# Spectral sums by accumulating transfers from GpSimd instead of load, add and store

## The chip, the core and the metric

The kernel runs on one core of one Trainium2 chip. The metric is the device time of one execution in microseconds (us). Of the kernel before, three runs took 2753.51 to 2755.38 us, the median is 2754.12 us. Engines are named as in the profile: PE (TensorE), DVE (VectorE), ACT (ScalarE), POOL (GpSimd) and SP (SyncE, which here issues transfers).

## The reference

Two independent results stand side by side in the output of 2048 x 2048 fp32. Columns 0 to 1023 are an attention with 32 heads that share one key and one value head:

```python
q = (x @ wq).reshape(B, S, H, Dh).transpose(0, 2, 1, 3)      # S 2048, H 32, Dh 32
k, v = x @ wk, x @ wv
p = softmax(einsum("bhqd,bkd->bhqk", q, k) * Dh ** -0.5)
a = einsum("bhqk,bkd->bhqd", p, v).transpose(0, 2, 1, 3).reshape(B, S, H * Dh) @ wo
```

Columns 1024 to 2047 are a Fourier mixing, the part that the change touches:

```python
a = einsum("bsd,ed->bse", x, dft_hid_re)
b = einsum("bsd,ed->bse", x, dft_hid_im)
y = einsum("ts,bse->bte", dft_seq_re, a) - einsum("ts,bse->bte", dft_seq_im, b)
```

## The kernel before

The large matrix products (both stages of the Fourier mixing, and the last product with `wo`) are done in Strassen's way: `PRODUCTS` (line 30) lists seven products of blocks in place of eight. Each takes a signed sum of left blocks and of right blocks, and its result goes with a sign into one or two of four result blocks. So most results are sums of several products, and each of the 12 entries (product, result block) past the first of its block is an addition to what stands there already.

Stage 1 (`stage_1`, line 381) makes the hidden transform in the order `ORDER_1` = 4, 1, 2, 3, 0, 6, 5; each product has 8 row blocks of 128 rows and 2 column halves, so 16 groups. Its sums are kept in DRAM tiles of 128 x 512 fp32 called `a` (256 KB each). Stage 2 (`stage_2`, line 405) multiplies by the sequence matrices in the order `ORDER_2` with 8 groups a product; its partial sums stand in DRAM tiles `y`, and the last addition goes into the output. Stage 3 is the product with `wo`.

A group accumulates in one of two PSUM banks (`psb`). Every operand is split into a high part (DVE: `mh`, `rh`) and a low part (POOL or DVE: `ml`, `rl`), and three matmuls make one exact product. When a group is done, `gather` (line 351) copies the bank to an SBUF tile `h` on DVE. `h` comes from a ring of three buffers (`hr`, `NHR` = 3). A first entry is stored from `h` by SP. A first entry with a minus sign is copied a second time, times -1 (line 368). For any other entry SP loads the old sum to a tile `y` (ring of four), POOL adds or subtracts `h` (line 377), and SP stores `y` (line 379). There are 128 such additions in stage 1 and 64 in stage 2.

The attention runs between these groups. PE computes rows of scores into `pss` (two buffers of 128 x 1024), DVE takes their maximum (`nm`, line 727), ACT takes the exponent with its sum, which frees the buffer (line 729); PE computes the scores again transposed (`pst`), ACT takes their exponent to `p`, and PE multiplies `p` by `v` in bursts. A row's PE pair waits for the exponent of the row but one before (`row_deps`, line 899).

The order of all instructions is set while the program is built. `Plan` (line 67) keeps for every engine but PE the tasks whose inputs it expects to be there, with guessed durations, and picks by priority; the main loop (line 1040) picks PE's next work against the same clock. Each engine then executes its list strictly in order, and waits on semaphores where an input or a buffer is late. A ring slot may be taken in the plan once the users of the slot three before are finished in the plan; which of the three buffers a new tile gets is settled when it is made (`Ring.make`, line 161). Line numbers in the trace are nearly all L58, the helper that records every instruction, so the trace is read by tile names.

Of the kernel before, what the change touches and what calls it, by code (L numbers as in the profile page):

```python
# [12 lines left out]
ALU = mybir.AluOpType  # L13
# [4 lines left out]
P = 128  # L18
S = 2048
D = 1024  # L20
H = 32
DH = 32
W = 512
# [20 lines left out]
EXTRA = 2  # L44
OVER = {"act": 0.1, "dve": 0.08, "pool": 0.06, "sp": 0.0}
LAG = {"act": 0.1, "dve": 0.1, "pool": 0.15, "sp": 0.3, "pe": 0.1}
ISSUE, RATE, FLIGHT = 0.42, 300.0, 3.0


class Ordered:  # L50
# [16 lines left out]
class Plan:  # L67
# [6 lines left out]
        self.port = {"dve": 0.0, "pool": 0.0}  # L74
        self.seq, self.dma = 0, 0.0

    def task(self, engines, us, emit, deps=(), prio=0.0, kb=0, order=(), into=None, port=False):
        if isinstance(engines, str):
            engines = ((engines, 0.0),)
        t = into or Task()  # L80
        t.engines, t.us, t.emit, t.prio, t.kb, t.port = engines, us, emit, prio, kb, port
        self.seq += 1
        t.seq = self.seq
        for kind, ds in ((0, deps), (1, order)):
            for d in ds:
                if d is None:
                    continue
                if d.end is None:
                    t.n += 1
                    d.outs.append((t, kind))  # L90
                else:
                    t.ready = max(t.ready, d.start if kind else d.end)
        if t.n == 0:
            self.learn(t)
        return t
# [23 lines left out]
    def run(self, until):  # L119
        while True:  # L120
            best = self.next()
            if best is None or best[0] > until:
                return
            at, e = best
            r, t = min((x for x in self.known[e] if x[0] <= at), key=lambda x: (x[1].prio, x[1].seq))
            for f, _ in t.engines:
                self.known[f] = [x for x in self.known[f] if x[1] is not t]
            t.on = e
            t.emit(e) if len(t.engines) > 1 else t.emit()
            us = t.us[e] if isinstance(t.us, dict) else t.us  # L130
            if e == "pool" or (e == "dve" and t.port):
                at = max(at, self.port["dve" if e == "pool" else "pool"])
                self.port[e] = at + us - OVER[e]
            end = at + us
            self.free[e] = max(end - OVER[e], at + us / 2)
            if e == "sp":
                self.dma = max(self.dma, end) + t.kb / RATE
                end = self.dma + FLIGHT
            self.finish(t, at, end)


class Slot:
# [45 lines left out]
def tile_kernel(ctx: ExitStack, tc, xT, wq, wkv, wo, xbT, wT, cT, out):  # L188
# [3 lines left out]
    dve = Ordered(tc, nc.vector)  # L192
    gp = Ordered(tc, nc.gpsimd)
    sp = Ordered(tc, nc.sync)
    eng = {"act": act, "dve": dve, "pool": gp}
    scale = float(DH) ** -0.5
    plan = Plan()
# [7 lines left out]
    def scratch(name, shape=(P, W)):  # L205
        return dram.tile(list(shape), F32, name=name)
# [8 lines left out]
    y_d = [[[scratch(f"y_{t}_{e}_{k}") for k in range(8)] for e in range(2)] for t in range(2)]  # L215
# [27 lines left out]
    yr = Ring(misc, "y", NY, [P, W], F32)  # L243
    hr = Ring(misc, "h", NHR, [P, W], F32)
# [15 lines left out]
    def maker(ring, *a, **k):  # L260
        t = plan.task(*a, order=ring.maker, **k)
        ring.maker = [t]
        return t


    landed = defaultdict(Task)

    def store(to, of, deps, prio, kb=256, key=None, bits=False):
        return plan.task("sp", ISSUE, lambda: (move if bits else sp.dma_start)(to(), of()), deps=deps, prio=prio, kb=kb,
                         into=landed[key] if key else None)  # L270
# [71 lines left out]
    def totals():  # L342
        total = {}
        for _, _, outs in PRODUCTS:
            for i, j, _ in outs:
                total[i, j] = total.get((i, j), 0) + 1
        return total

    TOTAL = totals()

    def gather(g, at, outs, neg=False):

        s = hr.take()

        def evict():
            h = hr.make(s)
            if neg:
                dve.tensor_scalar_mul(h, g.ps, -1.0)
            else:
                dve.tensor_copy(h, g.ps)  # L360
        e = g.freed = maker(hr, "dve", 0.69, evict, deps=[g.done, *s.deps], prio=-0.5)
        for sg, key, n, to, of in outs:
            if of is None and sg > 0:
                s.users.append(store(to, lambda: s.tile, [e], at, key=(*key, n)))
                continue
            if of is None:
                s2 = hr.take()
                g.freed = maker(hr, "dve", 0.69, lambda s2=s2: dve.tensor_scalar_mul(hr.make(s2), g.ps, -1.0),
                                deps=[g.done, *s2.deps], prio=-0.5)
                s2.users.append(store(to, lambda s2=s2: s2.tile, [g.freed], at, key=(*key, n)))  # L370
                continue
            ys = yr.take()
            ld = plan.task("sp", ISSUE, lambda ys=ys, of=of: sp.dma_start(yr.make(ys), of()),
                           deps=[landed[*key, n - 1], *ys.deps], prio=at - 30, kb=256, order=yr.maker)
            yr.maker = [ld]
            f = gp.tensor_add if sg > 0 else gp.tensor_sub
            ad = plan.task("pool", 1.33, lambda ys=ys, f=f: f(ys.tile, ys.tile, s.tile), deps=[e, ld], prio=at - 20)
            s.users.append(ad)
            ys.users.append(store(to, lambda ys=ys: ys.tile, [ad], at, key=(*key, n)))

    def stage_1():
        seen = {}
# [22 lines left out]
    def stage_2():  # L405
        seen = {}
        for p in ORDER_2:
            at, bt, outs = PRODUCTS[p]
            R = [Item([(lambda r=r, e=e, c=c: a_d[r][e][c], sg) for r, e, sg in bt],
                      after=[("a", c // 8, r, c % 8, e, TOTAL[c // 8, r]) for r, e, sg in bt],  # L410
                      sums=scratch(f"as_{p}_{c}") if len(bt) > 1 else None) for c in range(NC)]
            for m in range(8):
                L = [Item([(lambda r=r, i=i, c=c, m=m: cT[r, i * 8 + m, :, c * 4:c * 4 + 4], sg) for r, i, sg in at])
                     for c in range(4)]
                got = []
                for i, j, sg in outs:
                    n = seen[i, j, m] = seen.get((i, j, m), 0) + 1
                    r0 = (i * 8 + m) * P
                    to = out[r0:r0 + P, D + j * W:D + (j + 1) * W] if n == TOTAL[i, j] else y_d[i][j][m]
                    got.append((sg, ("y", i, j, m), n, lambda to=to: to,  # L420
                                (lambda i=i, j=j, m=m: y_d[i][j][m]) if n > 1 else None))
                yield Group(L, R, lambda g, at, got=got: gather(g, at, got))

    def wo_set(e):
# [91 lines left out]
    rest = x_groups(1, False, True) + x_groups(2, False, True) + x_groups(3, False, True)  # L516
    rest += list(stage_1())
    rest += list(stage_2())
    WO = sum(g.n for g in start + rest)
    rest += list(stage_3())  # L520
# [321 lines left out]
    def at_of(deps):  # L842

        t = 0.0
        for d in deps:
            if d is None:
                continue
            if d.end is None:
                return None
            t = max(t, d.end + LAG["pe"])  # L850
        return t
# [17 lines left out]
    def product_deps(g, j):  # L869
        c, w = divmod(j, 3)  # L870
        l, r = g.left[c // 4], g.right[c]
        deps = [l.ready[0], r.ready[0]] if w == 0 else [r.ready[1]] if w == 1 else [l.ready[1]]
        if j == 0:
            deps.append(bank_task[other_bank()])
            deps += [o.done for o in odds if o.must <= fill]
        return deps
# [22 lines left out]
    def row_deps(s):  # L899
        u = s // SU  # L900
        return [*unit[u].open, *(kvs[:6] if s < EARLY else kvs), *([rexp[s - 2]] if s > 1 else [])]
# [14 lines left out]
    def col_deps(n):  # L916
        return [*unit[n // SU].rows, *([cexp[n - 1]] if n else [])]
# [11 lines left out]
    def pv_deps(k):  # L929
        u, q = flat[k]  # L930
        return [cexp[u * SU + 2 * bursts[u][q][1] - 1], bank_task[other_bank()]]
# [49 lines left out]
    def place():  # L981
        g = at_group[fill]
        return g, fill - g.at
# [40 lines left out]
    s = k = 0  # L1024
# [14 lines left out]
    n, after_burst, spare_0 = 0, False, None  # L1039
    while n < total:  # L1040
# [11 lines left out]
        elif k < len(flat) and n >= scored(k):  # L1052
            t = at_of(pv_deps(k))
# [13 lines left out]
        if after_burst:  # L1067
            after_burst = False
            t = at_of(row_deps(s)) if SU + LEAD <= s < min(n + SU + LEAD + RUN, total) else None
# [4 lines left out]
        if n and fill < BODY:  # L1074
            if spare_0 is None:
                spare_0 = spare()
            if spare() > spare_0 * (total - n) / total + SPARE_END:
                t = at_of(product_deps(*place()))
# [3 lines left out]
        if s >= min(n + SU + LEAD, total) and n < scored(k) + (held[0] is not None):  # L1082
            t = at_of(col_deps(n))
# [5 lines left out]
        if s < min(n + SU + LEAD + RUN, total) and (s >= SU + LEAD or fill >= min(s_at(s), BODY)):  # L1089
            t = at_of(row_deps(s))  # L1090
# [6 lines left out]
        if fill < BODY:  # L1097
            t = at_of(product_deps(*place()))
# [96 lines left out]
```

## Time and profile before

| | us |
|---|---|
| median of three runs | 2754.12 |
| the profiled execution, its own time | 2754.33 |
| its span from first to last instruction | 2752.5 |
| PE busy in the span | 2736.0 |
| ACT, DVE, POOL busy | 2199.5, 1944.1, 1579.5 |
| POOL's additions of spectral sums (192) | 249.3 |

The profiled execution lies within the three runs. PE is busy nearly all the time at a granted clock of 0.999, so an engine's busy time tells little: what counts is whether PE ever waits. Stage 1 of the Fourier part lies between about 350 and 1027 us, stage 2 between 1027 and 2480 us, and stage 3 and the end follow. Within stage 1, the third product (2) has its 16 groups between about 545 and 640 us.

### The profile page before, as it was taken

To read this page: it belongs to the slowest core of one execution; us is meant where nothing else is said; L and a number is where in the kernel's file an instruction comes from. 1 tells how busy PE (TensorE), PEld (TensorE's weight loads), DVE (VectorE), ACT (ScalarE), POOL (GpSimd) and SP (SyncE) were. 2 spreads that over 40 slices of the span, in tenths; PEclk is the share of its full clock that TensorE was granted. 3 is DMA by queue.
4 is the path that set the end of the run, shared out by engine and by line. 5 is a ranking of instruction groups with operands and counts; after the bars stand their busy time and mean duration, and the time that the engine had idled before them with its cause. 6 is when DMAs were issued, how large, how long until landed. Compare 5 with 4: busy or idle time off the path is not lost.

```text
span 2752.5 us, 40883 instructions
## 1 busy us (share of the span) xinstructions
PE 2736.0 (99%) x13832; PEld 1930.3 (70%) x13832; DVE 1944.1 (71%) x2277; ACT 2199.5 (80%) x3197; POOL 1579.5 (57%) x1307
## 2 busy tenths in 40 slices
PE   9999999999999999999999999999999999999999
PEld 6777676767676767677677676676676776766766
DVE  8977676768777776676677677677677676678752
ACT  6688887878787878888888888888888888887631
POOL 2644245557776557556346356557768767555562
PEclk9999999999999999999999999999999999999999
DMA  9645366567786548547437445547858857444585
GB/s 279 210 135 159 104 202 207 191 231 256 249 257 222 169 149 281 171 133 250 141 106 249 143 136 174 154 153 254 272 182 279 278 161 238 127 127 153 160 277 176
DMA packets 337043, 536.48 MB, mean 195 GB/s; under 512 B 36800, under 2 KB 89536, under 8 KB 336832
## 3 DMA queue, kind: packets, MB, share of 16 engines
q1 hardware_dynamic: 336832, 533.87, 61.3%
q8 instruction: 108, 1.77, 0.3%
q14 instruction: 103, 0.84, 0.1%
HBM read 390.86 MB, written 141.82 MB: 194 GB/s over the span
## 4 chain that ended last, share of the span: by engine, by line
PE 97%; ACT 1%; DVE 1%; DMA 1%; issue 0%; POOL 0%; SPq 0%; ACTq 0%; DVEq 0%
PE psb L58 62%; PE pss L58 18%; PE pst L58 17%; ACT pss L58 0%; ACT p L58 0%; DMA qst<-in_xT_dram 0%; DVE h L58 0%; DMA ql<-y 0%; DVE nm L58 0%; DVE rl L58 0%; DMA m<-in_wkv_dram 0%; DVE y L58 0%; ACT h L58 0%; POOL rl L58 0%; DVE p L58 0%
## 5 line engine op out<-in xcount | busy, mean ns | idle before, releaser
L58 DVE TENSOR_REDUCE nm<-pss 128x1 f32<-128x1024 f32 x1024 | 1241.6, 1221 | 325.0 <-PE pss L58 321.2
L58 ACT ACTIVATE p<-pst 128x1024 f32<-128x1024 f32 x1024 | 1052.5, 1028 | 448.6 <-PE pst L58 397.7
L58 ACT ACTIVATE pss<-pss,nm 128x1024 f32<-128x1024 f32 x1024 | 1110.7, 1085 | 35.0 <-DVE nm L58 33.6
L58 POOL TENSOR_TENSOR ml<-m,mh 128x512 fp32r<-128x512 f32 x371 | 482.6, 1301 | 508.2 <-DVE mh L58 290.9
L58 PE MATMUL psb<-rl,mh 128*128 128x512 f32 x1732 | 683.3, 395 | 0.6 <-POOL rl L58 0.6
L58 PE MATMUL psb<-rh,mh 128*128 128x512 f32 x1732 | 683.7, 395 | 0.2 <-DVE y L58 0.2
L58 PE MATMUL psb<-rh,ml 128*128 128x512 f32 x1732 | 683.3, 394 | 0.0
L58 PE MATMUL pss<-kst,qst 128*128 128x512 f32 x2048 | 650.4, 398 | 0.9 <-ACT pss L58 0.9
L58 PE MATMUL pst<-qst,kst 128*128 128x512 f32 x2048 | 642.8, 395 | 2.4 <-ACT p L58 2.2
L58 PEld LDWEIGHTS pss<-kst,qst 128*128 128x128 f32 x2048 | 375.6, 188 | 163.6 <-issue 72.9
L58 PE MATMUL psb<-p,v 128*32 128x512 f32 x4096 | 461.8, 596 | 2.7 <-DVE h L58 2.7
L58 PEld LDWEIGHTS pst<-qst,kst 128*128 128x128 f32 x2048 | 382.5, 188 | 103.1 <-ACT p L58 8.6
L58 POOL TENSOR_TENSOR m<-m,m 128x512 f32<-128x512 f32 x230 | 301.0, 1309 | 152.4 <-DMA m<-in_cT_dram 93.8
L58 PEld LDWEIGHTS psb<-rh,mh 128*128 128x128 f32 x1732 | 324.9, 188 | 77.7 <-DVE y L58 0.6
L58 PEld LDWEIGHTS psb<-rl,mh 128*128 128x128 f32 x1732 | 324.9, 188 | 76.6 <-POOL rl L58 1.0
L58 PEld LDWEIGHTS psb<-rh,ml 128*128 128x128 f32 x1732 | 324.9, 188 | 75.7
L58 POOL TENSOR_TENSOR y<-y,h 128x512 f32<-128x512 f32 x192 | 249.3, 1306 | 176.8 <-DVE h L58 165.1
L58 PEld LDWEIGHTS psb<-p,v 128*32 128x32 f32 x4096 | 122.7, 110 | 286.5 <-issue 273.7
L58 POOL TENSOR_TENSOR rl<-r,rh 128x512 fp32r<-128x512 f32 x198 | 255.7, 1299 | 117.6 <-DVE rh L58 108.5
L58 DVE TENSOR_REDUCE mh<-m 128x512 fp32r<-128x512 f32 x371 | 250.7, 676 | 20.5 <-PE psb L58 13.8
L58 ACT ACTIVATION_READ_ACCUMULATOR pss<-pss,nm 128x1 f32 x1024 | 208.2, 203 | 0.0
L58 POOL TENSOR_TENSOR r<-r,r 128x512 f32<-128x512 f32 x140 | 180.5, 1293 | 47.8 <-DMA r<-a 31.1
(78 smaller groups left out, 977.0 us busy)
## 6 DMA issues: line engine op xcount, KB each, us to landing
m<-in_cT_dram SPq DMA_DIRECT2D x384, 256.0 KB, 3.8
r<-a SPq DMA_DIRECT2D x192, 256.0 KB, 4.2
y<-a SPq DMA_DIRECT2D x128, 256.0 KB, 3.7
a<-y SPq DMA_DIRECT2D x128, 256.0 KB, 3.2
r<-in_wT_dram SPq DMA_DIRECT2D x96, 256.0 KB, 3.9
m<-in_xbT_dram SPq DMA_DIRECT2D x96, 256.0 KB, 3.3
y<-y SPq DMA_DIRECT2D x96, 256.0 KB, 4.1
as<-r SPq DMA_DIRECT2D x80, 256.0 KB, 4.4
```

Of the source, the lines that this page charges most:

```text
L58: return lambda *a, **k: self.tc.keep_in_program_order(f(*a, **k))
```

## The change

Additions to a sum that stands in DRAM are no longer made by load, add and store. GpSimd issues one transfer per addition, which reads the SBUF tile `h` and adds it to the DRAM tile (`accum_op=ALU.add`). Where the entry has a minus sign, DVE makes a second copy of the bank, times -1, in another slot of the `h` ring, and that tile is added. In stage 2 all entries go straight into the output; the DRAM tiles `y` are not used. The plan takes 1.0 us on POOL for such a task (`ACC`) and regards its result as landed, and the `h` slot as free, `FLIGHT + 1.0` = 4 us later. The rest is as it was.

```diff
-ISSUE, RATE, FLIGHT = 0.42, 300.0, 3.0
+ISSUE, RATE, FLIGHT, ACC = 0.42, 300.0, 3.0, 1.0
...
-            self.finish(t, at, end)
+            self.finish(t, at, end + t.after)
...
-            ys = yr.take()
-            ld = plan.task("sp", ISSUE, lambda ys=ys, of=of: sp.dma_start(yr.make(ys), of()),
-                           deps=[landed[*key, n - 1], *ys.deps], prio=at - 30, kb=256, order=yr.maker)
-            yr.maker = [ld]
-            f = gp.tensor_add if sg > 0 else gp.tensor_sub
-            ad = plan.task("pool", 1.33, lambda ys=ys, f=f: f(ys.tile, ys.tile, s.tile), deps=[e, ld], prio=at - 20)
-            s.users.append(ad)
-            ys.users.append(store(to, lambda ys=ys: ys.tile, [ad], at, key=(*key, n)))
+            if sg < 0:
+                s2 = hr.take()
+                e2 = g.freed = maker(hr, "dve", 0.69, lambda s2=s2: dve.tensor_scalar_mul(hr.make(s2), g.ps, -1.0),
+                                     deps=[g.done, *s2.deps], prio=-0.5)
+            else:
+                s2, e2 = s, e
+            s2.users.append(plan.task("pool", ACC, lambda s2=s2, to=to: gp.dma_start(to(), s2.tile, accum_op=ALU.add),
+                                      deps=[e2, landed[*key, n - 1]], prio=at - 20, into=landed[*key, n], after=FLIGHT + 1.0))
...
-                    to = out[r0:r0 + P, D + j * W:D + (j + 1) * W] if n == TOTAL[i, j] else y_d[i][j][m]
+                    to = out[r0:r0 + P, D + j * W:D + (j + 1) * W]
```

With other durations the plan comes out in another order. Two places in product 2 of stage 1 show it, where every group is stored once with plus (tile `a_0`) and added once with minus (tile `a_1`). In these rows the numbers tell tiles apart; DMAHW0 to 7 are semaphores of SP's transfers, DMASW0 to 7 those of POOL's.

The first place is DVE about the groups of row blocks 13 and 14. Before, each group has one copy `h`:

```order
L58 TENSOR_REDUCE nm_6067<-pss_6111 128x1 [waits PE_49]
L58 TENSOR_REDUCE nm_6067<-pss_6133 128x1 [waits PE_49]
L58 COPY h_6151<-psb_6103 128x512 [waits DMAHW3_49,PE_49]
L58 COPY mt_6160<-psb_6149 48x128 [waits PE_49]
L58 TENSOR_REDUCE nm_6067<-pss_6153 128x1 [waits PE_49]
L58 TENSOR_REDUCE mh_6189<-m0_5876 128x4x128
L58 TENSOR_TENSOR ov_5960<-ov_5960,psb_6165 128x512 [waits PE_49]
L58 TENSOR_REDUCE nm_6067<-pss_6202 128x1 [waits PE_49]
L58 TENSOR_REDUCE nm_6067<-pss_6210 128x1 [waits PE_49]
L58 TENSOR_REDUCE nm_6067<-pss_6233 128x1 [waits PE_49]
L58 COPY h_6249<-psb_6215 128x512 [waits DMAHW5_49,PE_49]
L58 TENSOR_REDUCE nm_6067<-pss_6252 128x1 [waits PE_49]
```

Now each has two, the second one times -1 (TENSOR_SCALAR):

```order
L58 TENSOR_SCALAR h_6113<-psb_6042 128x512 [waits DMAHW2_49,DVE_49]
L58 TENSOR_REDUCE mh_6119<-m0_5836 128x4x128
L58 TENSOR_REDUCE nm_5997<-pss_6116 128x1 [waits PE_49]
L58 COPY h_6154<-psb_6099 128x512 [waits DMASW2_49,DVE_49,PE_49]
L58 TENSOR_SCALAR h_6161<-psb_6099 128x512 [waits DMASW3_49,DVE_49]
L58 TENSOR_TENSOR ov_5907<-ov_5907,psb_6133 128x512 [waits PE_49]
L58 TENSOR_REDUCE nm_5997<-pss_6164 128x1 [waits PE_49]
L58 TENSOR_REDUCE nm_5997<-pss_6191 128x1 [waits PE_49]
L58 COPY h_6206<-psb_6172 128x512 [waits DMASW4_49,DVE_49,PE_49]
L58 TENSOR_SCALAR h_6212<-psb_6172 128x512 [waits DMAHW7_49]
```

A group's copies have come to two, and the second copies `h_6161` and the next first copy `h_6206` wait for semaphores of POOL's transfers. The second place is POOL beside it. Before, POOL adds `h` to a loaded `y`:

```order
L58 TENSOR_TENSOR m0_6091<-m0_6091,m1_6096 128x512 [waits DMAHW1_49,DMAHW0_49,Pool_49]
L58 TENSOR_TENSOR y_5974<-y_5974,h_6151 128x512 [waits DMAHW6_49,DMAHW2_49,DVE_49]
L58 TENSOR_TENSOR ml_6190<-m0_5876,mh_6189 128x512 [waits DVE_49,PE_49]
L58 TENSOR_TENSOR m0_6198<-m0_6198,m1_6200 128x512 [waits DMAHW4_49,DMAHW3_49,Pool_49]
L58 TENSOR_TENSOR y_6070<-y_6070,h_6249 128x512 [waits DMAHW6_49,DVE_49]
L58 TENSOR_TENSOR y_6130<-y_6130,h_6287 128x512 [waits DMAHW7_49,DVE_49]
L58 TENSOR_TENSOR ml_6306<-m0_5951,mh_6305 128x512 [waits DVE_49,PE_49]
```

Now it issues a transfer of the negated tile, each on the next of eight semaphores (it waits there for the transfer eight before):

```order
L58 TENSOR_TENSOR m0_6048<-m0_6048,m1_6056 128x512 [waits DMAHW3_49,DMAHW1_49,Pool_49]
L58 DMA a_1_1_13_243<-h_6113 128x512 [waits DMASW3_49,DVE_49]
L58 TENSOR_TENSOR ml_6120<-m0_5836,mh_6119 128x512 [waits DVE_49,PE_49]
L58 DMA a_1_0_14_228<-h_6161 128x512 [waits DMASW4_49,DVE_49]
L58 TENSOR_TENSOR m0_6156<-m0_6156,m1_6159 128x512 [waits DMAHW2_49,DMAHW0_49,Pool_49]
L58 DMA a_1_1_14_244<-h_6212 128x512 [waits DMASW5_49,DVE_49]
L58 TENSOR_TENSOR ml_6228<-m0_5899,mh_6227 128x512 [waits DVE_49,PE_49]
```

The addition's place in POOL's list is taken by the transfer; the one of `h_6113` uses DMASW3, that of `h_6161` DMASW4, so those are what the two DVE copies above wait for.

## Rows read from the trace of the kernel before

**Rows 1.** The page's first lines: the span, and engines' busy time and instructions.

```profile
span 2752.5 us, 40883 instructions
...
PE 2736.0 (99%) x13832; PEld 1930.3 (70%) x13832; DVE 1944.1 (71%) x2277; ACT 2199.5 (80%) x3197; POOL 1579.5 (57%) x1307
```

**Rows 2.** The page's chain that ended last, shares by engine.

```profile
PE 97%; ACT 1%; DVE 1%; DMA 1%; issue 0%; POOL 0%; SPq 0%; ACTq 0%; DVEq 0%
```

**Rows 3.** Stretches: length, busy PE, PEld, DVE, ACT, POOL, clock, DMA share, GB/s.

```profile
545.00:640.00 95.00, 95.00 (x496) 65.69 (x495) 67.54 (x80) 76.55 (x111) 57.60 (x47) 1.00 0.70 230
640.00:1027.00 387.00, 385.47 (x1951) 273.02 (x1953) 286.06 (x331) 315.29 (x457) 263.32 (x217) 1.00 0.68 218
```

**Rows 4.** Costliest groups, whole run: busy us, mean ns, idle before, releaser.

```profile
L58 DVE TENSOR_REDUCE nm<-pss 128x1 f32<-128x1024 f32 x1024 | 1241.6, 1221 | 325.0 <-PE pss L58 321.2
...
L58 POOL TENSOR_TENSOR y<-y,h 128x512 f32<-128x512 f32 x192 | 249.3, 1306 | 176.8 <-DVE h L58 165.1
```

**Rows 5.** Groups of DVE between 545 and 640 us.

```profile
L58 DVE TENSOR_REDUCE nm<-pss 128x1 f32<-128x1024 f32 x37 | 44.8, 1219 | 12.5 <-PE pss L58 12.5
...
L58 DVE COPY h<-psb 128x512 f32<-128x512 f32 x16 | 11.0, 690 | 4.3 <-issue 1.9 <-PE psb L58 1.4 <-DMA qst<-ql 0.5
L58 DVE TENSOR_REDUCE mh<-m 128x512 fp32r<-128x512 f32 x8 | 5.4, 674 | 0.0
...
L58 DVE TENSOR_TENSOR rl<-r,rh 128x512 fp32r<-128x512 f32 x4 | 3.3, 834 | 0.1
L58 DVE TENSOR_TENSOR ov<-ov,psb 128x512 f32<-128x512 f32 x3 | 2.1, 686 | 6.6 <-PE psb L58 6.6
```

**Rows 6.** DMA, 545 to 640 us: busy tenths in 40 slices; issues, median landing.

```profile
DMA  6999999988996469748303236884492032659999
...
y<-a SPq DMA_DIRECT2D x16, 256.0 KB, 3.9
a<-h SPq DMA_DIRECT2D x16, 256.0 KB, 3.3
a<-y SPq DMA_DIRECT2D x16, 256.0 KB, 3.3
```

**Rows 7.** The page's DMA queues: packets, MB, share of 16 engines.

```profile
q1 hardware_dynamic: 336832, 533.87, 61.3%
```

**Rows 8.** Tile y: its stores' issue on SP, who waited for it, its landings.

```profile
L58 SPq DMA_DIRECT2D a<-y x128: 319/326/1330, 449.4 to 1028.1; - x128
...
  PEld psb L58: 0.6, 1
  PE psb L58: 0.2, 1
...
DMA to landing us min/median/max: 2.0/3.5/8.4
```

**Rows 9.** Waits, whole run: engine, tile, releaser; total, times, longest.

```profile
PEld psb L58 <- DVE h L58: 6.1, 11, 1.0
```

**Rows 10.** Timeline of DVE: start, duration, instruction, idle before.

```profile
619.22 1.23 DVE L58 TENSOR_REDUCE nm<-pss 128x1 f32<-128x1024 f32 x1 [1.58 <-PE pss L58]
620.38 0.69 DVE L58 COPY h<-psb 128x512 f32<-128x512 f32 x1
621.31 1.23 DVE L58 TENSOR_REDUCE nm<-pss 128x1 f32<-128x1024 f32 x1 [0.24 <-PE pss L58]
623.41 1.23 DVE L58 TENSOR_REDUCE nm<-pss 128x1 f32<-128x1024 f32 x1 [0.87 <-PE pss L58]
```

**Rows 11.** Timeline of POOL, the add behind that copy.

```profile
621.15 1.29 POOL L58 TENSOR_TENSOR y<-y,h 128x512 f32<-128x512 f32 x1 [2.30 <-DVE h L58]
```

**Rows 12.** Timeline of ACT, the exponent of that row.

```profile
620.84 1.08 ACT L58 ACTIVATE pss<-pss,nm 128x1024 f32<-128x1024 f32 x1
621.83 0.20 ACT L58 ACTIVATION_READ_ACCUMULATOR pss<-pss,nm 128x1 f32 x1
```

**Rows 13.** Timeline of PE, the pair of products for the next row but one.

```profile
622.74 0.62 PE L58 MATMUL pss<-kst,qst 128*128 128x512 f32 x2
```

More of the change, by code (lines that the diff above doesn't have):

```diff
@@ L75, in __init__, with task @@
         self.seq, self.dma = 0, 0.0
-    def task(self, engines, us, emit, deps=(), prio=0.0, kb=0, order=(), into=None, port=False):
+    def task(self, engines, us, emit, deps=(), prio=0.0, kb=0, order=(), into=None, port=False, after=0.0):
         if isinstance(engines, str):
@@ L80, in task @@
         t = into or Task()
-        t.engines, t.us, t.emit, t.prio, t.kb, t.port = engines, us, emit, prio, kb, port
+        t.engines, t.us, t.emit, t.prio, t.kb, t.port, t.after = engines, us, emit, prio, kb, port, after
         self.seq += 1
@@ L418, in stage_2 @@
                     r0 = (i * 8 + m) * P
-                    to = out[r0:r0 + P, D + j * W:D + (j + 1) * W] if n == TOTAL[i, j] else y_d[i][j][m]
+                    to = out[r0:r0 + P, D + j * W:D + (j + 1) * W]
                     got.append((sg, ("y", i, j, m), n, lambda to=to: to,
-                                (lambda i=i, j=j, m=m: y_d[i][j][m]) if n > 1 else None))
+                                True if n > 1 else None))
                 yield Group(L, R, lambda g, at, got=got: gather(g, at, got))
```

## The prediction

> **What bounds the kernel now.** I read the page's engine shares first, then the chain of waits, then a table of busy time by stretches, the groups, the transfers, and last the timeline of the stretch that the change touches most. PE is busy for 2736.0 of 2752.5 us [rows 1], and the chain that ended last is PE for 97%, with ACT, DVE and DMA at 1% each [rows 2]. So nothing that runs beside PE can shorten the kernel; all that can be won is the 16.5 us in which PE is idle, and most of that has nothing to do with the spectral sums. What can happen is a loss: PE has no spare time in which it would catch up. From 545 to 640 us, where product 2 of stage 1 runs, it is busy for 95.00 of 95 us, with DVE at 67.54 and POOL at 57.60; in the rest of stage 1 it is busy 385.47 of 387 us [rows 3]. The question is thus only whether the new order of waits makes PE wait.
>
> **What is removed.** POOL's 192 additions were 249.3 us at 1306 ns [rows 4]. They were beside PE: all that PE and its weight loads ever waited for tile y is 0.6 + 0.2 us [rows 8]. SP loses 192 loads and 192 stores of 256 KB. The hardware queue took 61.3% of 16 engines' span for 533.87 MB [rows 7]; 256 KB (0.262 MB) is therefore 2752.5 x 0.613 x 0.262 / 533.87 = 0.83 us of all engines, and 384 of them are 318 us. Each is worth nothing by itself, since PE doesn't wait there. Gain: at most the 0.8 us. If all of PE's waits for DVE's copies went too, it would be 6.1 us more [rows 9], but those copies stay.
>
> **What is added, and hidden.** POOL issues 192 transfers. If an issue takes as long as the addition did (1.3 us), POOL's list is as full as before; SP's issue of a store took 0.33 us [rows 8], so 0.33 is the lower end. The work queued behind it (`ml`, `rl`, sums of operands) stood behind the addition before, which waited for the same copy on DVE. On the DMA engines an accumulating transfer reads two things and writes one; if it costs no more than the load and the store that it replaces, the load on them is the same 0.70 share as in this stretch before [rows 3]. The 24 negated copies (16 in product 2, 8 in stage 2) are 24 x 0.69 = 16.5 us of DVE, of which 16 x 0.69 = 11 us fall into a stretch in which DVE has 95 - 67.5 = 27.5 us free.
>
> **What is added on the path.** A copy `h` was free as soon as POOL had added it; now it is free when the transfer has landed, and the next copy into that buffer waits for this on DVE. Behind that copy in DVE's list stand the row maxima `nm`, behind those the exponents on ACT, and behind those PE's next pair for a row. This is the new wait that I price.
>
> How long a buffer is held, from the end of the copy to landing: POOL started its add 0.1 us after the copy's end (620.38 + 0.69 to 621.15) [rows 10, 11]. The issue is 0.33 to 1.31 us, and I take 1.3, as for POOL's own add. No accumulating transfer is in the trace. A store of `a` landed in 3.3 us and a load in 3.9 in this stretch, both one after the other 7.2 [rows 6]; the longest landing of any transfer of y was 8.4 [rows 8]. Reading and writing overlap within a transfer, and the DMA engines are at 9 tenths in parts of the stretch, so I take the middle between 3.3 and 7.2, 5.3. Hold time: 0.1 + 1.3 + 5.3 = 6.7 us; lower end 0.1 + 0.33 + 3.3 = 3.7, upper end 0.1 + 1.3 + 8.4 = 9.8.
>
> How much time the order leaves for it: in product 2 every group takes two of three buffers, and the second copy's buffer is often the one that a transfer was only just given. Between `h_6113` and `h_6161`, which waits for the former's transfer, stand `mh`, one `nm` and one copy: 0.67 + 1.22 + 0.69 = 2.6 us [rows 5]. Between `h_6161` and `h_6206`: `ov` and two `nm`, 0.69 + 2 x 1.22 = 3.1 us. Worked out in the same way, the other pairs of that product leave 5.0, 5.2, 6.4 and 6.9 us, then five between 7.0 and 8.0 (there with the time at which a row's maximum could start in the trace). In products with one addition a group the gap is above 11 us, and with two additions a group it is 9.7 us and more; in stage 2 groups come every 26 us.
>
> At 6.7 us of hold the waits are 4.1, 3.6, 1.7, 1.5 and 0.3 us. Part is absorbed: DVE idles 0.87 us before a maximum [rows 10], ACT starts the exponent 0.39 us after the maximum's end (620.45 to 620.84), and PE's pair comes 0.71 us after the exponent's sum is read (622.03 to 622.74) [rows 10, 12, 13]; together 1.97 us, less 0.69 for the negated copy itself, so about 1.3 us for each wait. Left are 2.8 + 2.3 + 0.4 + 0.2 = 5.7 us. At the lower end (3.7 us) the waits are 1.1 and 0.6, and nothing is left. At the upper end (9.8 us) they are 7.2, 6.7, 4.8, 4.6, 3.4, 2.9 and five of 1.8 to 2.8, of which 27 us are left.
>
> Sum, on the profiled execution: 2752.5 + 5.7 of span, and the 1.8 us that lay around it, 2754.33 - 2752.5. That is 2760.0; the median of the runs is 0.2 us below the profiled one, so I say **2760**.
>
> **Rivals.** (a) The transfers land soon enough. Then the two short gaps cost less than the slack, and the time stays at 2754 to 2757. For it: stores in this stretch take 3.3 us, and a hold time up to about 5 us leaves only 1.1 + 0.6 = 1.7 us. It decides below 6.5 us of hold, where 5 us or less are left. Against it: an addition has to fetch the old sum first, and the same DMA engines run at 9 tenths. The Trainium skill speaks for it (DMA: Bandwidth & Descriptors, section on the anatomy of one DMA on the GpSimd path): about 2.0 us fixed plus the bytes over 436 GB/s, which as an estimate is 2.6 us for 256 KB and would make the hold time 4.0 us and the loss nothing. Here even plain transfers landed later than that, at 3.3 and 3.9 us [rows 6], so the page's price is given no weight of its own.
>
> (b) The transfers are much slower, because POOL needs several us for an issue or the addition in flight runs at a fraction of a copy's rate. At a hold of 12 us each of the eleven gaps costs 2.2 us more than at 9.8: 27 + 24 = 51, and the 32 groups with two additions start to wait as well; 2805 or more. For it: nothing in the trace shows such a transfer, and two per group of 5 us would take all POOL has. Against: a plain landing was never over 8.4 us.
>
> (c) It gets faster: with 384 transfers fewer, operands are early, PE's waits for copies and sums go, 0.8 + part of 6.1, so 2750. For it is only the length of SP's list; PE waits for transfers nowhere in stages 1 and 2, where it is idle for 1.6 us of 482 from 545 to 1027 [rows 3].
>
> **How the numbers follow.** The forecast (hold about 6.5 to 10 us) has 0.48, (a) 0.33, (b) 0.14, (c) 0.05. A difference of 0.2% is 5.5 us, about what a measurement of this kernel can tell from no change. The forecast is just past this bound; of its 0.48 I count 0.38 as slower and 0.10 as the same. With (b) slower has 0.52. The same has 0.10 + 0.30 + 0.02 = 0.42, faster 0.03 + 0.03 = 0.06. The range goes from 2752, a little below (a), to 2786, a little above the upper end of 2754 + 27; (b)'s far part and (c)'s good part, 0.15 or so, lie outside.
>
> **What would show it.** Right: on DVE, waits of `h` for POOL's or the a-transfers of 2 to 5 us at a handful of places between 545 and 640 us and nearly none elsewhere; PE idle about 5 us more in that stretch, which grows by as much; a landing of POOL's transfers near 5 us and an issue near 1.3. Wrong: waits of that kind beside a PE that is not later (the slack is larger); the loss in another stretch, at the start of stage 2 or through `ml` or `rl` from POOL; a hold under 5 us or over 10.

## The result and the profile after

The changed kernel takes 2758.82 us, the median of 20 runs (2756.77 to 2763.12), against 2754.07 us of the kernel before in the same comparison (20 runs, 2751.84 to 2758.45). The ratio is 1.0017, with a 95% interval of 1.0010 to 1.0024: slower by 4.7 us, a little less than the 0.2% that was named as the bound. The forecast was 2760. The ratio given with each kernel here is taken over runs that compare, so it is not always the quotient of the two medians beside it.

The page of the changed kernel, its span and the engines' busy time, answers to [rows 1]:

```profile
span 2758.0 us, 40447 instructions
PE 2738.1 (99%) x13832; PEld 1929.8 (70%) x13832; DVE 1941.9 (70%) x2290; ACT 2199.4 (80%) x3197; POOL 1515.8 (55%) x1318
```

The span is 5.5 us longer. PE has the same 13832 products; its busy time grew by 2.1 us and its idle time from 16.5 to 19.9 us, by 3.4. The stretches say where PE is idle (length, busy PE, PEld, DVE, ACT, POOL, clock, DMA share, GB/s; the first two answer to [rows 3]):

```profile
545.00:640.00 95.00, 92.84 (x458) 66.05 (x457) 72.88 (x91) 73.24 (x107) 48.31 (x45) 0.98 0.74 178
640.00:1027.00 387.00, 386.02 (x1961) 270.38 (x1960) 272.69 (x320) 314.39 (x457) 231.38 (x223) 1.00 0.74 154
1027.00:2480.00 1453.00, 1451.27 (x7454) 1014.89 (x7454) 1023.49 (x1164) 1236.42 (x1792) 861.57 (x732) 1.00 0.62 179
```

The last stretch before, for comparison:

```profile
1027.00:2480.00 1453.00, 1452.93 (x7459) 1018.21 (x7452) 1023.51 (x1162) 1240.56 (x1798) 884.36 (x730) 1.00 0.61 191
```

Product 2 (545 to 640 us) went from no idle PE to 2.16 us, and its clock from 1.00 to 0.98. The rest of stage 1 has 0.98 us idle in place of 1.53, stage 2 1.73 in place of 0.07. That is +2.16 - 0.55 + 1.66 = 3.3 us of idle time. But the stretches are cut at fixed times, and one wait crosses the cut at 1027 us. It is the same product in both kernels, PE's 5033rd (5032 have started before it), first before and then now:

```profile
1025.36 1.49 PE L58 MATMUL psb<-p,v 128*32 128x512 f32 x12 [0.68 <-DVE h L58]
```

```profile
1030.34 1.50 PE L58 MATMUL psb<-p,v 128*32 128x512 f32 x12 [0.68 <-DVE h L58]
```

Counted where it belongs, the rest of stage 1 has 1.66 us idle in place of 1.53, and stage 2 1.05 in place of 0.07.

A product with the same number is also a better mark than a time. PE's 2601st product, just ahead of product 2, starts at 543.98 us before and at 543.74 now. From there to the 5033rd PE takes 481.38 us before and 486.60 now: stage 1 loses 5.2 us, more than what is seen as idle time. From there to the 12401st product, at 2459.87 us before and 2467.02 now, 2.2 us more are lost, and the end gives 1.7 back; the clock below says why.

**Product 2.** DVE's waits for transfers of `h` in this stretch are two (engine and tile, releaser: total us, times, longest):

```profile
DVE h L58 <- DMA a<-h: 6.2, 2, 4.1
```

The first of them, on DVE (start, duration, instruction, idle before):

```profile
553.55 0.68 DVE L58 TENSOR_SCALAR h<-psb 128x512 f32<-128x512 f32 x1
554.28 0.69 DVE L58 COPY h<-psb 128x512 f32<-128x512 f32 x1
554.89 1.22 DVE L58 TENSOR_REDUCE nm<-pss 128x1 f32<-128x1024 f32 x1
...
561.99 0.69 DVE L58 TENSOR_SCALAR h<-psb 128x512 f32<-128x512 f32 x1 [4.10 <-DMA a<-h]
```

and the chain of waits through it (start, length, what):

```profile
554.53 7.36 DMA a<-h
...
561.99 0.70 DVE h L58
...
562.73 1.43 PE psb L58 x5
```

The negated copy at 553.55 filled a buffer; POOL issued its transfer at 554.53, which landed 7.36 us later; the next negated copy got the same buffer, and until it was made the PSUM bank that it reads was not free. So PE did not wait for a row, as I had it, but for the bank:

```profile
562.73 0.50 PE L58 MATMUL psb<-rh,mh 128*128 128x512 f32 x1 [2.16 <-DVE h L58]
```

Behind the idle time the granted clock fell to its lower level for some 3 us (stretches of 2 us, columns as above):

```profile
564.00:566.00 2.00, 2.00 (x6) 1.56 (x5) 2.00 (x3) 1.49 (x3) 1.17 (x1) 0.52 0.80 138
566.00:568.00 2.00, 2.00 (x7) 1.57 (x6) 0.29 (x2) 1.72 (x3) 1.78 (x2) 0.62 1.05 244
```

That is 2 x 0.48 + 2 x 0.38 = 1.7 us lost with PE busy. The place cost 2.2 + 1.7 = 3.9 us in this execution.

But the kernel before has such a fall too, near its end, behind 0.88 and 1.17 us of idle PE (between 2695 and 2698 us):

```profile
2698.00:2700.00 2.00, 2.00 (x10) 0.61 (x14) 0.69 (x1) 1.02 (x1) 1.42 (x2) 0.50 0.99 340
2700.00:2702.00 2.00, 2.00 (x16) 0.44 (x12) 0.13 (x1) 0.00 (x0) 0.86 (x1) 0.66 0.74 229
```

It costs 2 x 0.50 + 2 x 0.34 = 1.7 us as well, and the changed kernel, with the same two idle times there, keeps its clock at 1.00. So the clock is no part of the 5.5 us, and the 2.1 us by which PE's busy time grew are not the clock's; in which products they lie is not shown.

The second wait is at the pair `h_6113`, `h_6161` of the prediction, and PE never noticed it: between 612 and 636 us it was busy throughout.

```profile
620.65 0.69 DVE L58 TENSOR_SCALAR h<-psb 128x512 f32<-128x512 f32 x1 [2.15 <-DMA a<-h]
```

```profile
612.00:636.00 24.00, 24.00 (x125) 16.49 (x124) 18.10 (x23) 17.81 (x27) 9.96 (x10) 1.00 0.64 148
```

**Why that transfer was late.** The DMA engines from 548 to 564 us (busy tenths in 40 slices; issues and median landing):

```profile
DMA  9989967999999999999999999999999999998410
...
a<-h POOLq DMA_DIRECT2D x3, 256.0 KB, 6.8
qst<-qh SPq DMA_DIRECT2D x2, 256.0 KB, 7.8
```

They were full: loads of the attention's `qst` and of operands were under way beside it, and among the packets recorded on its queue none moves between its issue and 558.5 us. That the backlog held it up is argued from this, not shown.

**The transfers themselves.** POOL's group in stage 1 (busy us, mean ns) and the page's issues (KB, us from the start of the issue to landing) and queues (packets, MB, share of 16 engines):

```profile
L58 POOL DMA_DIRECT2D a<-h x128 | 115.9, 996 | 135.5 <-DVE h L58 125.8 <-DVE mt L58 4.6 <-DVE nm L58 3.3
```

```profile
a<-h POOLq DMA_DIRECT2D x128, 256.0 KB, 5.0
```

```profile
q1 hardware_dynamic: 281536, 433.18, 50.2%
q0 software_dynamic: 27648, 50.34, 12.6%
```

One addition keeps the 16 engines busy for 2758.0 x 0.126 / 192 = 1.81 us. The load and the store that it replaces took 2 x 0.83 = 1.66 us by [rows 7]. Fewer bytes thus bring no relief: 50.2 + 12.6 = 62.8% of the span is busy now, 61.3% before.

**Product 3.** The rest of stage 1 lost an idle time of 0.67 us of before (at 859 us) and got others, 0.32 us at 663 and 0.46 at 668. POOL now waits longer for operands between 640 and 1027 us, first before and then now:

```profile
POOL m L58 <- DMA m<-in_xbT_dram: 3.4, 4, 1.2
```

```profile
POOL m L58 <- DMA m<-in_xbT_dram: 29.7, 11, 5.8
```

Most of it is hidden. The chain to the stall at 663 us goes from a transfer, issued behind four others on SP, over POOL's list and DVE's `rh` to a row's maximum, the exponent and PE's pair, the path that the prediction had priced for product 2. In POOL's list stand a wait of 2.96 us for an operand, up to 652.30 us, and two issues of accumulating transfers (`POOL a x2`). Which of them decides is not shown.

```profile
651.15 2.88 DMA rb<-r
...
656.09 1.71 POOL a L58 x2
657.80 1.31 POOL ml L58
659.11 1.24 POOL r L58
...
660.37 0.69 DVE rh L58
661.06 1.14 DVE nm L58
...
662.28 1.21 ACT pss L58 x2
...
663.54 0.73 PE pss L58 x2
```

### The profile page after: what moved, and what is told of

It reads as the page before. It is cut to its first block, busy times and chain, and to the rows that moved or that the text cites. A ratio compares the mean times of both kernels' runs of the same rounds, so it can differ in the third digit from the quotient of the medians.

```text
span 2758.0 us, 40447 instructions
## 1 busy us (share of the span) xinstructions
PE 2738.1 (99%) x13832; PEld 1929.8 (70%) x13832; DVE 1941.9 (70%) x2290; ACT 2199.4 (80%) x3197; POOL 1515.8 (55%) x1318
## 3 DMA queue, kind: packets, MB, share of 16 engines
q1 hardware_dynamic: 281536, 433.18, 50.2%
q0 software_dynamic: 27648, 50.34, 12.6%
## 4 chain that ended last, share of the span: by engine, by line
PE 93%; DMA 2%; POOL 1%; ACT 1%; DVE 1%; issue 1%; SPq 0%; POOLq 0%; ACTq 0%; DVEq 0%
PE psb L58 59%; PE pss L58 18%; PE pst L58 16%; DMA m<-in_cT_dram 1%; ACT pss L58 1%; POOL ml L58 0%; DMA r<-a 0%; ACT p L58 0%; DVE nm L58 0%; DVE h L58 0%; SPq L58 0%; DMA a<-h 0%; POOL rl L58 0%; DMA qst<-in_xT_dram 0%; POOL r L58 0%
## 5 line engine op out<-in xcount | busy, mean ns | idle before, releaser
L58 POOL TENSOR_TENSOR ml<-m,mh 128x512 fp32r<-128x512 f32 x369 | 503.3, 1364 | 489.1 <-DVE mh L58 265.4
L58 POOL TENSOR_TENSOR rl<-r,rh 128x512 fp32r<-128x512 f32 x211 | 279.4, 1336 | 104.0 <-DVE rh L58 97.2
L58 POOL TENSOR_TENSOR r<-r,r 128x512 f32<-128x512 f32 x140 | 192.8, 1405 | 54.2 <-DMA r<-a 23.1
L58 POOL DMA_DIRECT2D a<-h x128 | 115.9, 996 | 135.5 <-DVE h L58 125.8
```

The costliest lines, as they stand in the source:

```text
L58: return lambda *a, **k: self.tc.keep_in_program_order(f(*a, **k))
```

## The experiments

Twelve kernels ran. Theory A: the loss is the copy that waited for a transfer from a buffer given out again too soon. Rival B: the additions load the DMA engines, and what is late is late whatever the buffers. Rival C: the other order of the plan. E and N are named where they come up.

**Both kernels again.** No edit.

> The kernel before, unchanged, for a second profile. If the small stalls of PE in stage 2 (0.4 to 1.6 us each, one to three of them, in the changed kernel and in all four variants so far, none over 0.3 us in the one profile of before) belong to the accumulating transfers, this profile has none again between 1035 and 2480 us. If they come by chance, as the one of 1.6 us in the variant whose stage 2 adds as before suggests, one or two stand here as well.

> The changed kernel, unchanged, a second time for a second profile. Theory A: the wait of a second copy for a transfer near 562 us is there again, 3 to 4.5 us, with PE idle 1.5 to 2.5 us; the clock behind it may or may not be lower (it was lower in one and not in the other of two profiles with this wait). 2758 to 2759.5.

Before: 2754.54 us (one run). Its profile repeats the first one: PE busy for 95.00 of 95 us in product 2, 1452.93 of 1453 us in stage 2, and 481.41 us from PE's 2601st to its 5033rd product, against 481.38. As far as two profiles tell, the stalls of PE there belong to the kernel and not to the run. After: 2758.62 us (11 runs), ratio 1.0016 (1.0007 to 1.0025). The wait near 562 us is there again, 3.3 us, with PE idle for 1.7 us; the clock was 1.00 this time, to the end of the kernel. Even so PE takes 486.16 us between the two products, 4.8 more than before. The waits in product 2:

```profile
DVE h L58 <- DMA a<-h: 6.9, 3, 3.3
...
PE psb L58 <- DVE h L58: 1.7, 1, 1.7
PE pss L58 <- ACT pss L58: 0.5, 1, 0.5
```

**Which stage.** One line ahead of the new branch keeps load, add and store for stage 1, or for stage 2:

```diff
+            if key[0] == "a":      # e3: "y"
+                ... load y, add on POOL, store y, as before
+                continue
```

> Stage 1 adds by load, add and store as before; only the 64 additions of stage 2 are accumulating transfers from GpSimd. Theory A: stage 2 has groups some 26 us apart, so no copy waits, and the time is that of the kernel before plus the 1 to 2 us by which PE was idle in stage 2 of the changed kernel (0.07 us before, 1.74 us after between 1027 and 2480 us): 2754 to 2756. Rival B (transfers load the DMA engines): about a third of the loss, 64 of 192, so 2755.7. Rival D (the loss belongs to stage 2 and the end): 2757 or more.

> Only the 128 additions of stage 1 are accumulating transfers; stage 2 loads, adds and stores as before. Theory A: the long wait in product 2 is still there, so 3.5 to 4.5 us over the kernel before, 2757.5 to 2758.5, with PE idle about 2 us near 560 us and a clock below 1.00 just behind it. Rival B: two thirds of the loss, 2757.2, without a single place for it. Rival D: 2754 to 2755.

Only stage 2: 2755.89 us, ratio 1.0008 (0.9999 to 1.0017). Only stage 1: 2758.97 us, 1.0017 (1.0008 to 1.0026). The times alone leave stage 2 a share between none and all of the loss. The profiles say more: from PE's 2601st to its 5033rd product the first takes 481.37 us, as before, the second 485.58, 4.2 more. So the changed stage 1 loses by itself most of what is lost there. The second one's profile has the wait again (4.0 us on DVE, PE idle 1.9 us); the clock behind it stayed at 1.00, against the expectation. It also has stalls behind 1027 us, PE idle for 2.5 us there (0.68 of it is the wait that crosses the cut), although stage 2 adds as before: what is lost in stage 2 can come from stage 1 and the plan's new order too.

**The buffers.** In strict turn, or the negated copy in another ring:

```diff
-        s.tile = pool.tile(shape, dtype or dt, name=name, bufs=self.bufs)
+            s.tile = pool.tile(shape, dtype or dt, name=name + "abcdef"[s.n % self.bufs], bufs=1)
```

```diff
-                s2 = hr.take()
-                e2 = g.freed = maker(hr, "dve", 0.69, lambda s2=s2: dve.tensor_scalar_mul(hr.make(s2), g.ps, -1.0),
+                s2 = yr.take()
+                e2 = g.freed = maker(yr, "dve", 0.69, lambda s2=s2: dve.tensor_scalar_mul(yr.make(s2), g.ps, -1.0),
```

> The changed kernel with one difference: the three buffers of the `h` ring are given out strictly in turn, so that a buffer comes round again after three copies and not after two or after one. The order of the engines' instructions is the same. Theory A (the loss is one copy on DVE that waited 4.1 us for a transfer issued only just before from the same buffer, 2.2 us of idle PE and about 1.7 us of PE at a lower clock behind it): no wait of DVE for a transfer of a<-h over 1 us between 545 and 640 us, PE there busy at a clock of 1.00, and 3 to 4 us less than the changed kernel, about 2755.0. Rival B (the accumulating transfers load the DMA engines, and what is late is late whatever the buffers): within 1 us of the changed kernel, 2758 to 2760. Rival C (the other order of the plan costs it, a little at many places): the same 2758 to 2760, with PE's idle time spread out.

> The changed kernel, but the negated copy goes into the ring `y` of four buffers, which nothing else uses in stages 1 and 2, so that `h` has one copy a group again. Theory A: a buffer of either ring comes round after more than 11 us, over any landing seen (at most 9.3 us), no copy waits for a transfer, and the time is 2754.5 to 2756. Rival B: 2758 to 2760 as the changed kernel. Rival C: anything between, with PE's idle time at other places.

Strict turn: 2757.32 us against 2754.86, ratio 1.0010 (1.0001 to 1.0019), between what A and B expected. The longest wait of a copy fell to 1.4 us, PE was idle for 0.17 us in product 2, and yet 2.5 of 4.7 us stayed; the intervals of the two kernels overlap, so half is what the medians say, not more. Its profile says where: from PE's 2601st to its 5033rd product it takes 482.60 us, so that 1.2 of 5.2 us of loss are left in stage 1, as A had it; from there to the 12401st it loses 4.4 us, twice what the changed kernel does, and why is open. The other ring: 2758.68 us, 1.0014 (1.0005 to 1.0023), no gain that could be measured, though no copy waited for a transfer at all; between the two products 484.56 us, so 3.2 of 5.2 us are left in stage 1. Here theory A misses. Some 3 us at 560 went another way: DVE's `rl`, which takes 0.68 us where POOL is idle beside it, took 3.82 while POOL worked without a break (DVE, then POOL and PE, start, duration, instruction, idle before):

```profile
558.68 3.82 DVE L58 TENSOR_TENSOR rl<-r,rh 128x512 fp32r<-128x512 f32 x1
562.42 2.34 DVE L58 TENSOR_REDUCE nm<-pss 128x1 f32<-128x1024 f32 x2
```

```profile
557.85 1.60 POOL L58 TENSOR_TENSOR ml<-m,mh 128x512 fp32r<-128x512 f32 x1
559.09 1.59 POOL L58 TENSOR_TENSOR rl<-r,rh 128x512 fp32r<-128x512 f32 x1
560.34 1.60 POOL L58 TENSOR_TENSOR r<-r,r 128x512 f32<-128x512 f32 x1
```

```profile
564.98 0.73 PE L58 MATMUL pss<-kst,qst 128*128 128x512 f32 x2 [1.43 <-ACT pss L58]
```

The Trainium skill (GPSIMD Engine Reference, section on specifications) says that GpSimd and VectorE share their way to SBUF, and that a VectorE instruction with two SBUF inputs collides there. The trace agrees: `rl` has two such inputs and ended 0.56 us after POOL's third instruction (562.50 and 561.94). In the kernel before, too, each of the 24 splits of this kind (`rl`, `ml`) on DVE with no POOL work beside it took 0.7 us, and those beside POOL's work between 0.7 and 4.4. This place has no room for 3 us on DVE, whoever brings them; the product-3 stall (0.8 us) was there too.

**A hold without any new transfer.** The kernel before, with eight copies for one at the second group of product 2:

```diff
+            for _ in range(hold):      # 7 for the group (2, 0, 1), else 0
+                dve.tensor_copy(h, g.ps)
```

> The kernel before with one edit: at the second group of product 2 of stage 1 DVE copies the bank to `h` eight times in place of once, so DVE and everything behind it is held for about 7 x 0.6 = 4.2 us at the place where the changed kernel's DVE waited 4.1 us. No accumulating transfer exists in it. Theory A (a hold of DVE there is what costs, by PE waiting for the bank or for the next row): PE idle 1.5 to 3 us near 560 us, with or without a lower clock behind it, and 2 to 4 us over the kernel before. The prediction's own slack of about 2 us leaves 4.2 - 2.0 = 2.2 us. Rival E (there is slack enough, and the changed kernel's loss needs the transfers): PE idle under 0.5 us there and the time of the kernel before.

2761.05 us against 2754.07, ratio 1.0025 (1.0016 to 1.0034): 7.0 us, above what either side expected. The hold came out as 5.76 - 0.68 = 5.1 us, not 4.2. DVE, PE, then the clock in stretches of 2 us:

```profile
552.33 5.76 DVE L58 COPY h<-psb 128x512 f32<-128x512 f32 x8
```

```profile
558.14 6.24 PE L58 MATMUL psb<-p,v 128*32 128x512 f32 x36 [4.67 <-DVE h L58]
```

```profile
556.00:558.00 2.00, 0.00 (x0) 0.00 (x0) 1.93 (x3) 0.00 (x0) 0.00 (x0) 0.50 0.53 200
558.00:560.00 2.00, 1.86 (x12) 0.55 (x16) 1.97 (x5) 0.00 (x0) 1.83 (x2) 0.50 0.35 131
560.00:562.00 2.00, 2.00 (x16) 0.44 (x12) 1.22 (x1) 0.00 (x0) 2.00 (x2) 0.50 0.95 349
```

PE idles for 4.67 of the 5.1 us, and then runs some 4 us at half clock. Of the 2 us of slack that the prediction took from the row path, 0.4 are there on this one: PE had next to nothing else to do before it needed the bank.

**The addition in the transfer.** The same transfers, issues, copies and buffers, without the adding:

```diff
-gp.dma_start(to(), s2.tile, accum_op=ALU.add)
+gp.dma_start(to(), s2.tile)
```

> The changed kernel, but GpSimd's 192 transfers write over the DRAM tile and add nothing to it (the spectral sums are left out). Issue on GpSimd, order, buffers and copies are the same; only what the DMA engines do in the transfer differs. Theory B (the reading and adding in the DMA engines is the load that hurts): the 12.6% of the engines' time on that queue falls to about 6%, landing from 5.0 to about 3.5 us, no wait of a copy over 1.5 us, and 2755 to 2756. Theory A (a buffer reused too soon plus a backlog of other loads in front of the transfer): the landing of the one late transfer stays above 6 us because it waits behind loads, the wait is 2.5 to 4 us, and the time 2757 to 2758.5.

2754.95 us against 2754.07, ratio 1.0005 (0.9996 to 1.0013). By the medians most of the loss is gone, as rival B had it; the interval overlaps a little with the changed kernel's. In stage 1 it is plain: from PE's 2601st to its 5033rd product it takes 482.49 us, so 1.1 of 5.2 us are left, and the product-3 stall is gone. The order of instructions on every engine is that of the changed kernel here. So rival C, the order by itself, can't be what loses the 5.2 us; of stage 2's 2.2 us 1.9 stay. Landing and queue:

```profile
a<-h POOLq DMA_DIRECT2D x128, 256.0 KB, 2.8
```

```profile
q0 software_dynamic: 15360, 50.34, 4.9%
```

The engines are busy 2754.7 x 0.049 / 192 = 0.70 us a transfer, not 1.81, and POOL issues in 0.56 us, not 0.88 (medians). The copy that waited for 4.1 us waits for 2.6 (its transfer landed after 4.7 us in place of 7.4, and theory A had expected over 6), and PE is idle there for 0.5 us. The Trainium skill (DMA: Bandwidth & Descriptors, section on the anatomy of one DMA on the GpSimd path), whose fit the prediction turned into an estimate of 2.6 us for rival (a), holds for this plain transfer (2.8); the adding one took 5.0, and that section has no price for it.

**The minus signs.** Load, subtract and store for the 24 minus additions, accumulating transfers for the other 168; once more with strict turn:

```diff
+            if sg < 0:
+                ... load y, subtract on POOL, store y, as before
+                continue
```

> The changed kernel, but the 24 additions with a minus sign (16 in product 2 of stage 1, 8 in stage 2) are made by load, subtract and store, without a negated copy; the other 168 stay accumulating transfers. Theory A: product 2 is as before, its two waits of copies go, and what is left is 1 us in product 3 and 1 to 2 us in stage 2: 2755.5 to 2757. Rival B (load on the DMA engines by all 192): seven eighths of the loss stay, 2758. Rival C (the plan's order): 2758 as well, at other places.

> The variant that keeps load, subtract and store for the 24 additions with a minus sign, measured a second time (2752.10 the first time, 2 us under the kernel before, the interval of the ratio 0.9989 to 1.0007). If it is really faster than both kernels: 2751 to 2753 again. If the first time was chance: 2753.5 to 2755.

> The variant that keeps load, subtract and store for the 24 additions with a minus sign, with the three `h` buffers also given out strictly in turn. If what was left of buffer waits mattered there, 1 us less than the same variant without it; since no copy waited over 0.3 us for a transfer in that one's profile, I expect the same, 2751.5 to 2753.

2752.10 us against 2754.07, ratio 0.9998 (0.9989 to 1.0007); again 2753.11 against 2754.16, 0.9999 (0.9990 to 1.0008); strict 2756.42 against 2754.16, 1.0002 (0.9993 to 1.0010). The loss is gone as far as these intervals tell, more than any of A, B and C had expected. The second measurement fell between the two times set for it, and strict turn, from which 2751.5 to 2753 was expected, gave runs from 2751.18 to 2757.55. None is faster than the kernel before beyond its interval, so no version here beats the kernel before. In product 2 PE is busy again throughout:

```profile
545.00:640.00 95.00, 95.00 (x496) 65.73 (x495) 70.14 (x81) 76.41 (x112) 55.87 (x46) 1.00 0.68 224
```

**The second copies alone.** The kernel before, with two copies where the changed kernel has a negated one:

```diff
+            if twice:      # a minus addition follows; the plan reckons 1.29 us
+                dve.tensor_copy(h, g.ps)
```

> The kernel before (load, add, store) in which DVE copies the bank twice into the same `h` for the 24 groups whose addition has a minus sign, and the plan reckons with 1.29 us in place of 0.69. It has the DVE time of the negated copies and the longer hold of the bank, but neither a second buffer nor a transfer that adds. Theory N (DVE's time for the second copies is itself what delays): 2 us or more over the kernel before, 2756 to 2758, with PE idle over 1 us between 545 and 640 us. Theory A (the wait of the second copy for a buffer and its transfer is what costs): 2754 to 2755, PE idle under 0.5 us there.

2754.47 us against 2754.16, ratio 1.0003 (0.9994 to 1.0012). DVE's time for the copies costs nothing that could be measured (PE idle for 0.79 us in product 2, a little over what A expected there; the time is inside its range).

## Why the prediction was right, and where it was not

**The bound and the kind of loss: right.** PE is the bound, all that was removed was worth nothing, and what the new wait cost it was not got back. SP's 384 transfers and POOL's additions gave no time: 168 of 192 additions as accumulating transfers leave the kernel where it was (0.9998 and 0.9999). The 318 us on the DMA engines came out as 61.3% of 2752.5 less 50.2% of 2758.0 = 303 us saved and 348 us added, a little worse than the even exchange assumed.

**The place: right, but not all of it.** The 24 minus additions carry the loss, and the longest wait stands in product 2, with the `h` buffers that come round too soon. I expected PE to be idle there for some 5 us more and nearly nothing elsewhere; it was 2.2 us there, and 0.8 us of idle PE in product 3 and 1 us in stage 2 stand beside it. In the chain of the first stand late operands, a cost that I had set at nothing because the load on the engines would be the same, and POOL's issues; the second was not tied to the transfers (above).

**The hold: mis-sized for most, right for one.** The term was 0.1 + 1.3 + 5.3 = 6.7 us. Landing is counted from the start of an issue, in [rows 6] as well, so the issue's 1.3 us were counted twice. POOL's issue began 0.3 us after the copy's end, took 0.88 (median), and the landing was 5.0, and 4.2 in product 2. Of the sixteen holds of negated copies there twelve were 4.2 to 5.3 us, the median of all 4.5: the hold that I had given to rival (a), and under the 5 us that I had named as a sign of being wrong. So of eleven short gaps only two or three became waits. The pair of the 4.1 us wait stood among the mildest of the eleven, with a gap of 7 to 8 us, since I let the row's maximum between them start when rows started in the trace of before. DVE did that work sooner, so that the gap was 3.66 us of bare work (554.23 to 561.99 less the 4.10 us of wait), and the transfer, beside full DMA engines, landed 7.66 us after the copy's end (561.89 less 554.23). A gap that contains waiting can close, and a median landing says little of the one wait that costs.

**The slack: the path was wrong.** The prediction let each wait run over the row maximum, the exponent and PE's pair, and took off 1.3 us. Neither of the two waits behaved so. A copy also frees the PSUM bank that it reads. Where PE's next product needed that bank (562 us), what was taken off is what PE still had to do: of 4.1 us of wait 2.2 were idle PE, of 3.3 in the second profile 1.7, of 4.0 with stage 1 alone 1.9. That this takes off 1.6 to 2.1 us, not far from 1.3, is chance, for it has nothing to do with rows. Where the bank was not needed (620 us), all of 2.15 us was absorbed, a wait beside a PE that is not later, which I had named as a sign of being wrong. The hold experiment shows the first case with little to absorb: 4.67 us idle for 5.1 us of extra copies.

**The clock was not in the sum, and need not be.** Its fall behind the first idle time cost 1.7 us in one profile; in the second profile of the changed kernel, with 1.7 us of idle PE, and in that with stage 1 alone, with 1.9, it did not come there. The clock recorded with each run says that a fall comes in about half of the executions of either kernel: in the last comparison 16 of 33 before (mean 2755.1 us with it, 2753.0 without) and 6 of 11 after (2759.6 and 2757.9). With it as without it the change costs 4.5 to 4.9 us.

So the total of 5.7 us was near the 4.7 measured because errors cancelled: three waits too many and an issue counted twice on one side, and on the other a gap that closed, a bank in place of a row, late operands and a loss in stage 2. The forecast time was met in part by luck.

**What stays open.** The loss goes with the minus additions. In stage 1 it needs both the adding in the transfer and the buffer that comes round too soon: without either, 1.1 or 1.2 of 5.2 us are left, in one profile each. The other ring takes the early buffer away as well, but there the place lost its time to DVE's collision with POOL. Why the product-3 stall stays with the other ring and goes with strict turn and without the adding was not tried. Nor is it shown what loses some 2 us in stage 2, with the adding and without it.

## What to carry to other kernels

A copy out of PSUM gives back two things, its bank to the next product and, later, its own buffer: when you add a wait to it, ask first when PE needs that bank, because there the slack is only what PE still has to do until then (0.4 to 2.1 us here), while a wait elsewhere can be free. An accumulating transfer saves instructions and bytes, not DMA time: it took the engines 1.81 us for 256 KB, a little more than the load and the store, and held its source for 4.5 us (median in product 2) where an addition on POOL held it for some 1.4. So use it where its source has many us until it is needed again, and keep it out of the groups that take two buffers at once. To find where a few us of 2750 are lost, compare the start of the same product of the busy engine in both traces; idle time in stretches cut at fixed times misleads.

## What the runs showed of the hardware

- Adding in the transfer costs on three sides: 1.81 against 0.70 us of all DMA engines for 256 KB, 5.0 against 2.8 us from issue to landing, of which 0.88 against 0.56 us are the issue on POOL, with 144 packets a transfer against 80.
- One DVE instruction with two SBUF inputs stretched from 0.68 to 3.82 us beside three POOL instructions in a row.
- After 4.67 us without work PE ran at half its clock for some 4 us; after 2.2 us it did so for some 3. After 0.88 and 1.17 us near the end it did so in both profiles of the kernel before, and in neither of the changed kernel.
